# Feed-forward blocks of 512 tokens that run over the batch boundary, in a Fourier-mixing and ELU feed-forward kernel

## The chip, the core and the metric

The kernel runs on one core of a Trainium2 chip. A core has five engines that run beside each other: TensorE (PE, with its weight loads shown apart as PEld), VectorE (DVE), ScalarE (ACT), GpSimd (POOL) and SyncE (SP, which here only issues DMAs). Matrix products land in PSUM, from where DVE or ACT take them. The metric is the device time of one execution in microseconds.

## What is computed

The input is eight batches of 3,008 tokens with 256 features. Each batch goes through a Fourier transform along the tokens, a complex 256 x 256 product with bias, a soft threshold, and the inverse transform. The result, as 24,064 tokens in a row, goes through a feed-forward layer of 2,048 hidden features with an ELU.

```
X = rfft(x, axis=1)
Yr = Xr @ w_r - Xi @ w_i + b_r ;  Yi = Xr @ w_i + Xi @ w_r + b_i
Y* = sign(Y*) * max(|Y*| - 0.01, 0)
y = irfft(Yr + i Yi, n=3008, axis=1)
h = y.reshape(24064, 256) @ w_in
out = where(h > 0, h, exp(min(h, 0)) - 1) @ w_out
```

## The kernel before

**The transform** is done as matrix products, in units of work for one batch each:
- A (six units): first stage on the input tile `xt`; ACT copies the result out of PSUM, and after every second unit stores it to DRAM (`DA`).
- X (eight units): second stage, on `Z`, which SP loads from `DA`; ACT copies to `XT`.
- M (twelve units): the complex product; DVE adds the bias (L196), POOL does the soft threshold (L204, L205) into `Y`.
- B (six units): first stage of the inverse, from `Y`; ACT copies to `Bz` (L251), and after every second unit stores to DRAM (`DB`, L259).
- Y (eight units): last stage, from `Bs`, which SP loads from `DB` (`load_Bs`, L261, four loads, each for two Y units); ACT copies to `yT`, the transposed tokens of a batch, 752 tokens of one half of the features for each unit.

**The feed-forward** runs over blocks of up to 512 tokens, and for each block over eight pairs of 128 hidden features. One such pair is a *slot*, one turn of the loop at L826. A slot has a front, an ELU and a back:
- `front` (L675): four matmuls of `w_in_s` with 512 columns of `yT` into the PSUM tile `hps`; then ACT takes the exponential into `Et`. In a slot with an M unit ACT does two steps (L698, L699), in the others one (L701).
- `elu` and `finish_elu` (L706 to L727): DVE, with POOL in slots that hold no unit, clips `Et` and combines it with `hps` into `gT`. The combination is issued a slot later.
- `back` (L729): two slots after the front (LAG = 2), eight matmuls with 128 tokens of `gT` as the weights and `w_out_r` as the moving side, summed over the eight slots of a block in two PSUM tiles `ps_o`. After the eighth, ACT copies them to `osb` (L763, L767) and SP issues the output stores (L774). The next block uses the same two PSUM tiles.

A batch is cut into blocks by itself: 3,008 tokens are five blocks of 512 and one of 448, which are 48 slots (`PER`), 384 in all. In the block of 448 tokens the fronts have 448 columns and the eighth matmul of the back fills 64 rows of 128; all else is the same.

**The order of work** is written out by hand. While the feed-forward works on batch b, `plan(b)` (L783) lays one unit into a slot, ahead of the front: the rest of the Y units of batch b, then X, M and B of batch b+1, and A of batch b+2. The list `seq` starts at slot 0 (slot 1 for batch 0). With the two insertions, Y6 and Y7 stand at 20 and 24, M50 and M51 at 28 and 29, then A0, B4, A1, B5 and A2 to A5 at 30 to 37; A0 to A5 are dropped where there is no batch b+2. Y0 and Y1 of batch b+1 follow at slots 45 and 47 (`yn`). The `Bs` loads are issued in the slot of A2, the `Z` loads in that of A5, the input loads in slots 3, 8 and 13. All engines run their instructions in the order in which this loop issues them.

**PSUM**: two `hps` tiles (`psH`), one tile tagged `fps` (`psF`) that all units share, and the two `ps_o` tiles. In every third slot of a run of bare slots (slots without a unit) the front uses the `fps` tile as a third `hps`.

Of the kernel before, what the change touches and what calls it, by code (L numbers as in the profile page):

```python
# [9 lines left out]
AF = mybir.ActivationFunctionType  # L10
BF16 = mybir.dt.bfloat16
F32 = mybir.dt.float32
# [17 lines left out]
def kernel(  # L30
# [11 lines left out]
    nc = tc.nc  # L42
    P = nc.NUM_PARTITIONS

    B, S, D = x.shape
    assert D == 256 and S == N1 * N2
    DFF = moe_w_in.shape[1]
    E = moe_w_out.shape[1]
# [14 lines left out]
    w_in_s = constp.tile([P, 2, DFF], BF16, name="w_in_s")  # L63
# [24 lines left out]

    TB = 512
    NPAIR = NFT // 2  # L90
    NBLK = (S + TB - 1) // TB
    PER = NBLK * NPAIR
    LAG = 2
    n = B * PER
    WT = 2 * N1 * 8
# [10 lines left out]
    yT_of = {}  # L106
# [192 lines left out]
    with tc.tile_pool(name="stagep", bufs=1) as stagep:  # L299
# [12 lines left out]
        def mix(eng, a, sc, b, op0, op1, n=1):  # L312
            t = stagep.tile([P, n], F32, name=f"c{len(cols)}")
            cols.append(t)
            eng.scalar_tensor_tensor(t[:], a[:], sc, b[:], op0, op1)
            return t
# [73 lines left out]
        c1 = mix(dve, qcol, -2.0, pcol, ALU.mult, ALU.add)  # L390
        c0 = col(dve, c1, -1.0, ALU.mult, 1.0, ALU.add)
# [265 lines left out]
    for u in range(2):  # L657
# [9 lines left out]
    psO = ctx.enter_context(  # L667
        tc.tile_pool(name="psO", bufs=2, space=bass.MemoryType.PSUM, reuse_waits="tile")
    )
# [2 lines left out]
    g_of = {}  # L672
    po_of = {}

    def front(i, third, on_act):  # L675
        b, r = divmod(i, PER)
        blk, fp = divmod(r, NPAIR)
        bs = blk * TB
        nb = min(TB, S - bs)
        yT = yT_of[b]  # L680
        if third:
            hps = psF.tile([P, 2, TB], F32, name="hps", tag="fps")
        else:
            hps = psH.tile([P, 2, TB], F32, name="hps", tag="hps")
        for s in range(2):
            ft = 2 * fp + s
            for dt in range(2):
                nc.tensor.matmul(  # L688
                    hps[:, s, 0:nb], lhsT=w_in_s[:, dt, ft * P : ft * P + P],
                    rhs=yT[:, dt, bs : bs + nb], start=(dt == 0), stop=(dt == 1),  # L690
                )
        Et = late3.tile([P, 2, TB], F32, name="Et", tag="Et")
        E_ = Et[:, :, 0:nb]
        if i == n - 1:
            for s in range(2):
                nc.scalar.activation(E_[:, s], hps[:, s, 0:nb], AF.Exp)
        elif on_act:
            nc.scalar.activation(E_, hps[:, :, 0:nb], AF.Relu, scale=-1.0)  # L698
            nc.scalar.activation(E_, E_, AF.Exp, scale=-1.0)  # L699
        else:  # L700
            nc.scalar.activation(E_, hps[:, :, 0:nb], AF.Exp)  # L701
        return hps, Et, nb

    late_elu = []

    def finish_elu():  # L706
        for i, hps, Et, nb, whole in late_elu:
            E_, h_ = Et[:, :, 0:nb], hps[:, :, 0:nb]
            gT = late3.tile([P, 2, TB], F32R, name="gT", tag="gT")
            for s in range(2) if i == n - 1 else (slice(0, 2),):  # L710
                o, h, e = gT[:, s, 0:nb], h_[:, s], E_[:, s]
                if whole:
                    nc.vector.scalar_tensor_tensor(o, e, -1.0, h, ALU.add, ALU.max)  # L713
                else:
                    nc.vector.scalar_tensor_tensor(o, h, 0.0, e, ALU.max, ALU.add)  # L715
            g_of[i] = gT
        late_elu.clear()

    def elu(i, hps, Et, nb, on_pool, on_act):

        E_ = Et[:, :, 0:nb]
        if on_pool:
            for eng, s in ((nc.gpsimd, 1), (nc.vector, 0)):
                eng.tensor_scalar(E_[:, s], E_[:, s], 1.0, 0.0, ALU.min, ALU.max)  # L724
        elif not on_act:
            nc.vector.tensor_scalar(E_, E_, 1.0, -1.0, ALU.min, ALU.add)  # L726
        late_elu.append((i, hps, Et, nb, on_pool or on_act))  # L727

    def back(i):  # L729
        b, r = divmod(i, PER)  # L730
        blk, fp = divmod(r, NPAIR)
        bs = blk * TB
        nb = min(TB, S - bs)
        gT = g_of.pop(i)
        nsub = (nb + P - 1) // P
        if fp == 0:
            po_of[b, blk] = [
                psO.tile([P, 2, E], F32, name="ps_o", tag="outp") for _ in range((nsub + 1) // 2)
            ]
        po = po_of[b, blk]  # L740
        nq = (nsub + 1) // 2
        order = [(q, s) for q in range(nq) for s in range(2)]
        if i == n - 1:
            order = [(q, s) for s in range(2) for q in range(nq)]
        for q, s in order:
            ft = 2 * fp + s
            for i_ in range(2 * q, min(2 * q + 2, nsub)):
                t0, t1 = i_ * P, min(i_ * P + P, nb)
                nc.tensor.matmul(  # L749
                    po[q][0 : t1 - t0, i_ % 2, :], lhsT=gT[:, s, t0:t1],  # L750
                    rhs=w_out_r[:, ft, :], start=(ft == 0 and i_ % 2 == 0),
                    stop=(ft == NFT - 1), skip_group_check=True,
                )
        if fp < NPAIR - 1:
            return
        osb = late2.tile([P, 4, E], F32, name="osb", tag="osb")
        ov = out[b * S : b * S + S, :].rearrange("(r w j) e -> w r j e", w=4, j=8)
        last = i == n - 1
        for q in range(nq):
            k = min(2, nsub - 2 * q)  # L760
            copy = nc.vector.tensor_copy if last and q else nc.scalar.copy
            if nb >= (2 * q + k) * P:
                copy(osb[:, 2 * q : 2 * q + k, :], po[q][:, 0:k, :])  # L763
            else:
                for e in range(k):
                    rows = min(P, nb - (2 * q + e) * P)
                    copy(osb[0:rows, 2 * q + e, :], po[q][0:rows, e, :])  # L767
            for i_ in range(2 * q, 2 * q + k):
                t, end = bs + i_ * P, min(bs + i_ * P + P, bs + nb)
                while t < end:  # L770
                    w, r0 = t // WT, t % WT // 8
                    t1 = min(end, (w + 1) * WT)
                    p0, n8 = t - bs - i_ * P, (t1 - t) // 8
                    (nc.scalar if last and i_ % 2 == 0 else nc.sync).dma_start(  # L774
                        ov[w, r0 : r0 + n8], osb[p0 : p0 + 8 * n8, i_, :]
                    )
                    t = t1
        del po_of[b, blk]

    def put(kind, b, *a):  # L780
        return ({"A": unit_A, "X": unit_X, "M": unit_M, "B": unit_B, "Y": unit_Y}[kind], (b, *a))
# [1 line left out]
    def plan(b):  # L783

        f0 = [[] for _ in range(PER)]
        f1 = [[] for _ in range(PER)]
        n1, n2 = b + 1, b + 2
        mid = [("X", u) for u in range(8)] + [
# [4 lines left out]
        ]  # L793
        if n1 < B:
            lead, seq = int(b == 0), [("y", u) for u in range(2, 6)] + mid
            seq.insert(20, ("y", 6))
            seq.insert(24, ("y", 7))
            xs = (3, 8, 13)
            yn = (45, 47)
        else:  # L800
            lead, seq = 0, [("y", u) for u in range(2, 8)]
        for t, u in enumerate(seq, lead):
            if u[0] == "y":
                f0[t].append(put("Y", b, u[1]))
            elif u[0] == "A":
                if n2 < B:
                    f0[t].append(put("A", n2, u[1]))
            else:
                f0[t].append(put(u[0], n1, *u[1:]))
            if u == ("A", 2):  # L810
                f1[t] += [(load_Bs, (n1, w)) for w in range(4)]
            if u == ("A", 5) and n2 < B:
                f1[t] += [(load_Z, (n2, s0, s1)) for s0, s1 in ((0, 8), (8, NS))]
        if b == 0:
            f1[xs[0]].append((lambda: gate(Z_of[1][:, 16, 0:1]), ()))
        if n2 < B:
            for ci in range(3):
                f1[xs[ci]].append((load_x, (n2, ci)))
        if n1 < B:
            for u in range(2):  # L820
                f0[yn[u]].append(put("Y", n1, u))
        return f0, f1
# [3 lines left out]
    for i in range(n + LAG):  # L826
        if i < n:
            r = i % PER
            if r == 0:
# [7 lines left out]
            on_act = any(f is unit_M for f, a in f0[r])  # L837
            h = front(i, calm and bare % 3 == 2, on_act)
# [37 lines left out]
```

## Time and profile before

| | before |
|---|---|
| median of 3 runs | 941.27 us (941.2 to 941.69) |
| span of the profiled execution | 941.2 us |
| start of the slots, on PE | 59.5 us |
| slots | 384 |
| matmuls of the fronts (L688) | 1,536 |
| matmuls of the backs (L749) | 3,072 |
| HBM read and written | 55.31 MB, 49.81 MB |

The profile is of one execution. In its page and in the answers of the trace, a line such as `L749 PE MATMUL ps_o<-w_out_r,gT` names the line of the kernel, the engine, the operation, and what it writes and reads. "Busy" is the time in which an engine works on an instruction; matmuls overlap with each other, so a group's busy time is less than its count times the mean length of one, and the time from the start of one group to the start of the next tells better what it costs. In a timeline the columns are start and length in us, engine, line, operation, tiles, shapes and count, and in brackets the idle time of the engine ahead of it with what ended it.

### The profile page before, as it was taken

To read this page: it belongs to the slowest core of one execution; us is meant where nothing else is said; L and a number is where in the kernel's file an instruction comes from. 1 tells how busy PE (TensorE), PEld (TensorE's weight loads), DVE (VectorE), ACT (ScalarE), POOL (GpSimd) and SP (SyncE) were. 2 spreads that over 40 slices of the span, in tenths; PEclk is the share of its full clock that TensorE was granted. 3 is DMA by queue.
4 is the path that set the end of the run, shared out by engine and by line. 5 is a ranking of instruction groups with operands and counts; after the bars stand their busy time and mean duration, and the time that the engine had idled before them with its cause. 6 is when DMAs were issued, how large, how long until landed. Compare 5 with 4: busy or idle time off the path is not lost.

```text
span 941.2 us, 16753 instructions
## 1 busy us (share of the span) xinstructions
PE 914.0 (97%) x6583; PEld 644.5 (68%) x6583; DVE 735.0 (78%) x863; ACT 711.3 (76%) x818; POOL 265.6 (28%) x352
## 2 busy tenths in 40 slices
PE   8879999999999999999999999999999999999997
PEld 3447666776677666776667766777667766677775
DVE  7868677877788767886778866888678876788997
ACT  6657787787868788687787878778787878667664
POOL 6702430133310431205402143013331034221332
PEclk9999999999999999999999999999999999999999
DMA  8984217521283224722156021752128001321011
GB/s 261 362 235 142 85 46 216 163 68 46 90 224 109 68 64 122 213 92 88 49 170 206 27 90 45 208 170 68 45 82 232 23 23 55 106 65 42 23 46 43
DMA packets 90654, 106.20 MB, mean 113 GB/s; under 512 B 5264, under 2 KB 81296, under 8 KB 87216
## 3 DMA queue, kind: packets, MB, share of 16 engines
q1 hardware_dynamic: 43760, 57.16, 22.3%
q0 software_dynamic: 5968, 27.26, 8.9%
q10 hardware_dynamic: 40848, 20.71, 7.2%
q8 instruction: 51, 0.84, 0.4%
q14 instruction: 27, 0.22, 0.1%
HBM read 55.31 MB, written 49.81 MB: 112 GB/s over the span
## 4 chain that ended last, share of the span: by engine, by line
PE 49%; DVE 22%; ACT 17%; issue 5%; DMA 4%; ACTq 1%; DVEq 0%; POOL 0%; SPq 0%; POOLq 0%
PE hps L688 20%; PE ps_o L749 19%; DVE gT L713 10%; PE mps L189 5%; DVE gT L715 5%; ACT Et L701 5%; DVE Et L724 4%; ACT Et L698 3%; ACT osb L763 2%; ACT Bz L251 2%; DVE Et L726 2%; ACT A L126 2%; PE aps L143 2%; PE xps L174 2%; DVE yb L196 1%
## 5 line engine op out<-in xcount | busy, mean ns | idle before, releaser
L749 PE MATMUL ps_o<-w_out_r,gT 128*128 128x256 f32 (+1 forms) x3072 | 485.6, 301 | 1.3 <-DVE gT L713 0.5
L749 PEld LDWEIGHTS ps_o<-w_out_r,gT 128*128 128x128 f32 (+1 forms) x3072 | 405.9, 186 | 68.1 <-DVE gT L713 13.6
L688 PE MATMUL hps<-yT,w_in_s 128*128 128x512 bf16 (+1 forms) x1536 | 389.1, 375 | 8.8 <-DVE gT L715 5.0
L701 ACT ACTIVATE Et<-hps 128x1024 f32<-128x1024 f32 (+1 forms) x299 | 301.4, 1008 | 102.1 <-PE hps L688 81.1
L713 DVE SCALAR_TENSOR_TENSOR gT<-Et,hps 128x1024 fp32r<-128x1024 f32 (+2 forms) x187 | 220.0, 1177 | 62.3 <-ACT Et L699 44.7
L715 DVE SCALAR_TENSOR_TENSOR gT<-hps,Et 128x1024 fp32r<-128x1024 f32 (+1 forms) x198 | 240.2, 1213 | 17.6 <-DVE Et L726 0.9
L688 PEld LDWEIGHTS <-w_in_s 128*128 128x128 bf16 x1536 | 131.4, 98 | 146.8 <-issue 28.9
L726 DVE TENSOR_SCALAR Et<-Et 128x1024 f32<-128x1024 f32 (+1 forms) x198 | 136.0, 687 | 73.7 <-ACT Et L701 67.2
L204 POOL TENSOR_SCALAR clip<-yb 128x512 f32<-128x512 f32 x84 | 51.7, 616 | 339.2 <-DVE yb L196 277.9
L724 POOL TENSOR_SCALAR Et<-Et 128x512 f32<-128x512 f32 (+1 forms) x102 | 62.4, 612 | 280.6 <-ACT Et L701 279.4
L698 ACT ACTIVATE Et<-hps 128x1024 f32<-128x1024 f32 x84 | 86.5, 1029 | 67.5 <-PE hps L688 67.5
L205 POOL TENSOR_TENSOR Y<-yb,clip 128x512 bf16<-128x512 f32 x84 | 107.4, 1278 | 7.0
L196 DVE TENSOR_TENSOR yb<-mps,bias_bc 128x512 f32<-128x512 f32 x96 | 65.7, 688 | 34.3 <-PE mps L189 27.1
L699 ACT ACTIVATE Et<-Et 128x1024 f32<-128x1024 f32 x84 | 88.8, 1058 | 2.7
L126 ACT CAST XT<-xps 128x768 bf16<-128x768 f32 x61 | 49.1, 807 | 14.7 <-PE xps L174 14.7
L126 ACT CAST yT<-yps 128x752 bf16<-128x752 f32 x63 | 49.6, 788 | 13.2 <-PE yps L276 13.2
L189 PE MATMUL mps<-wcat_r,XT 128*128 128x512 bf16 x192 | 58.0, 384 | 0.6 <-ACT XT L126 0.6
L189 PE MATMUL mps<-wcat_s,XT 128*128 128x512 bf16 x192 | 57.1, 379 | 0.0
L724 DVE TENSOR_SCALAR Et<-Et 128x512 f32<-128x512 f32 (+1 forms) x102 | 56.1, 550 | 0.5 <-ACT Et L701 0.4
L126 ACT CAST A<-aps 128x1024 bf16<-128x1024 f32 x45 | 45.4, 1012 | 11.8 <-PE aps L143 11.6
L189 PEld LDWEIGHTS <-XT 128*128 128x128 bf16 x384 | 30.6, 98 | 29.5 <-ACT XT L126 0.9
L763 ACT COPY osb<-ps_o 128x512 f32<-128x512 f32 x88 | 47.2, 587 | 2.8 <-PE ps_o L749 2.8
(103 smaller groups left out, 400.5 us busy)
## 6 DMA issues: line engine op xcount, KB each, us to landing
xt<-in_x_dram POOLq DMA_DIRECT2D x21, 1024.0 KB, 5.4
out_dram<-osb SPq DMA_DIRECT2D x158, 128.0 KB
Bs<-DB SPq DMA_DIRECT2D x32, 384.0 KB
DB<-Bz ACTq DMA_DIRECT2D x21, 512.0 KB
DA<-A ACTq DMA_DIRECT2D x18, 512.0 KB
Z<-DA SPq DMA_DIRECT2D x7, 1152.0 KB
Z<-DA SPq DMA_DIRECT2D x11, 384.0 KB
xt<-in_x_dram POOLq DMA_DIRECT2D x6, 512.0 KB, 5.9
```

The lines of the kernel that those rows point to most:

```text
L126: nc.scalar.copy(dst, src)
L189: nc.tensor.matmul(ps, lhsT=XT[:, dt, c, o : o + P], rhs=wm[:, dt, :], start=(m == 0 and dt == 0), stop=(m == 1 and dt == 1),)
L205: nc.gpsimd.tensor_tensor(Y_of[b, q][:, i, :], yb[:], clip[:], ALU.subtract)
L688: nc.tensor.matmul(hps[:, s, 0:nb], lhsT=w_in_s[:, dt, ft * P : ft * P + P], rhs=yT[:, dt, bs : bs + nb], start=(dt == 0), stop=(dt == 1),)
L698: nc.scalar.activation(E_, hps[:, :, 0:nb], AF.Relu, scale=-1.0)
L699: nc.scalar.activation(E_, E_, AF.Exp, scale=-1.0)
L701: nc.scalar.activation(E_, hps[:, :, 0:nb], AF.Exp)
L713: nc.vector.scalar_tensor_tensor(o, e, -1.0, h, ALU.add, ALU.max)
L715: nc.vector.scalar_tensor_tensor(o, h, 0.0, e, ALU.max, ALU.add)
L724: eng.tensor_scalar(E_[:, s], E_[:, s], 1.0, 0.0, ALU.min, ALU.max)
L726: nc.vector.tensor_scalar(E_, E_, 1.0, -1.0, ALU.min, ALU.add)
L749: nc.tensor.matmul(po[q][0 : t1 - t0, i_ % 2, :], lhsT=gT[:, s, t0:t1], rhs=w_out_r[:, ft, :], start=(ft == 0 and i_ % 2 == 0), stop=(ft = ...
```

## The change

Blocks no longer end with a batch. The 24,064 tokens are cut into 47 blocks of 512, so there are 376 slots, and `PER`, the slots for each batch in the plan, is 47. A block that holds a batch boundary takes its front columns from two `yT` tiles: `pieces` cuts a stretch of tokens at the boundaries, and the front runs its matmuls for each piece, each with its own weight load, into the piece's columns of the same PSUM tile. There are seven such blocks; the pieces have 448 + 64, 384 + 128, 320 + 192, 256 + 256, 192 + 320, 128 + 384 and 64 + 448 tokens. The back always runs eight full matmuls. Output stores are cut at batch boundaries too.

In the plan, B4 and B5 move to slots 30 and 31, ahead of A0 to A5, which take 32 to 37; Y0 and Y1 of the next batch move to slots 38 and 39; the `Bs` loads move to the slot of A1 (33). Since 47 slots are not a multiple of 8, the ends of blocks fall on another slot of the plan in each batch.

```
-    NBLK = (S + TB - 1) // TB
-    PER = NBLK * NPAIR
+    assert S * NPAIR % TB == 0 and S % (P // 2) == 0
+    PER = S * NPAIR // TB
...
+    def pieces(t, k):
+
+        out_, c = [], 0
+        while c < k:
+            b, r = divmod(t + c, S)
+            e = min(k, c + S - r)
+            out_.append((b, r, c, e))
+            c = e
+        return out_
...
-        b, r = divmod(i, PER)
-        blk, fp = divmod(r, NPAIR)
-        bs = blk * TB
-        nb = min(TB, S - bs)
-        yT = yT_of[b]
+        blk, fp = divmod(i, NPAIR)
...
-            for dt in range(2):
-                nc.tensor.matmul(
-                    hps[:, s, 0:nb], lhsT=w_in_s[:, dt, ft * P : ft * P + P],
-                    rhs=yT[:, dt, bs : bs + nb], start=(dt == 0), stop=(dt == 1),
-                )
+            for b, t0, c0, c1 in pieces(blk * TB, TB):
+                for dt in range(2):
+                    nc.tensor.matmul(
+                        hps[:, s, c0:c1], lhsT=w_in_s[:, dt, ft * P : ft * P + P],
+                        rhs=yT_of[b][:, dt, t0 : t0 + c1 - c0],
+                        start=(dt == 0), stop=(dt == 1),
+                    )
...
-            for i_ in range(2 * q, min(2 * q + 2, nsub)):
-                t0, t1 = i_ * P, min(i_ * P + P, nb)
+            for i_ in range(2 * q, 2 * q + 2):
                 nc.tensor.matmul(
-                    po[q][0 : t1 - t0, i_ % 2, :], lhsT=gT[:, s, t0:t1],
+                    po[q][:, i_ % 2, :], lhsT=gT[:, s, i_ * P : i_ * P + P],
...
+            copy(osb[:, 2 * q : 2 * q + 2, :], po[q][:])
+            for i_ in range(2 * q, 2 * q + 2):
+                for b, t, c0, c1 in pieces(bs + i_ * P, P):
+                    ov = out[b * S : b * S + S, :].rearrange("(r w j) e -> w r j e", w=4, j=8)
+                    while c0 < c1:
+                        w, r0 = t // WT, t % WT // 8
+                        k = min(c1 - c0, (w + 1) * WT - t)
+                        (nc.scalar if last and i_ % 2 == 0 else nc.sync).dma_start(
+                            ov[w, r0 : r0 + k // 8], osb[c0 : c0 + k, i_, :]
+                        )
+                        t, c0 = t + k, c0 + k
...
-            ("M", 4, 1), ("B", 3), ("M", 5, 0), ("M", 5, 1), ("A", 0), ("B", 4), ("A", 1),
-            ("B", 5), ("A", 2), ("A", 3), ("A", 4), ("A", 5),
+            ("M", 4, 1), ("B", 3), ("M", 5, 0), ("M", 5, 1), ("B", 4),
+            ("B", 5), ("A", 0), ("A", 1), ("A", 2), ("A", 3), ("A", 4), ("A", 5),
...
-            yn = (45, 47)
+            yn = (38, 39)
...
-            if u == ("A", 2):
+            if u == ("A", 1):
                 f1[t] += [(load_Bs, (n1, w)) for w in range(4)]
```

More of the change, by code (lines that the diff above doesn't have):

```diff
@@ L686, in front @@
             ft = 2 * fp + s
-            for dt in range(2):
-                nc.tensor.matmul(
-                    hps[:, s, 0:nb], lhsT=w_in_s[:, dt, ft * P : ft * P + P],
-                    rhs=yT[:, dt, bs : bs + nb], start=(dt == 0), stop=(dt == 1),
-                )
+            for b, t0, c0, c1 in pieces(blk * TB, TB):
[5 more added lines that the diff above has]
+                    )
         Et = late3.tile([P, 2, TB], F32, name="Et", tag="Et")
-        E_ = Et[:, :, 0:nb]
+        E_ = Et[:]
         if i == n - 1:
             for s in range(2):
-                nc.scalar.activation(E_[:, s], hps[:, s, 0:nb], AF.Exp)
+                nc.scalar.activation(E_[:, s], hps[:, s], AF.Exp)
         elif on_act:
-            nc.scalar.activation(E_, hps[:, :, 0:nb], AF.Relu, scale=-1.0)
+            nc.scalar.activation(E_, hps[:], AF.Relu, scale=-1.0)
             nc.scalar.activation(E_, E_, AF.Exp, scale=-1.0)
         else:
-            nc.scalar.activation(E_, hps[:, :, 0:nb], AF.Exp)
-        return hps, Et, nb
+            nc.scalar.activation(E_, hps[:], AF.Exp)
+        return hps, Et
     late_elu = []
     def finish_elu():
-        for i, hps, Et, nb, whole in late_elu:
-            E_, h_ = Et[:, :, 0:nb], hps[:, :, 0:nb]
+        for i, hps, Et, whole in late_elu:
             gT = late3.tile([P, 2, TB], F32R, name="gT", tag="gT")
             for s in range(2) if i == n - 1 else (slice(0, 2),):
-                o, h, e = gT[:, s, 0:nb], h_[:, s], E_[:, s]
+                o, h, e = gT[:, s], hps[:, s], Et[:, s]
                 if whole:
@@ L717, in finish_elu, with elu @@
         late_elu.clear()
-    def elu(i, hps, Et, nb, on_pool, on_act):
-        E_ = Et[:, :, 0:nb]
+    def elu(i, hps, Et, on_pool, on_act):
+        E_ = Et[:]
         if on_pool:
@@ L726, in elu @@
             nc.vector.tensor_scalar(E_, E_, 1.0, -1.0, ALU.min, ALU.add)
-        late_elu.append((i, hps, Et, nb, on_pool or on_act))
+        late_elu.append((i, hps, Et, on_pool or on_act))
     def back(i):
-        b, r = divmod(i, PER)
-        blk, fp = divmod(r, NPAIR)
+        blk, fp = divmod(i, NPAIR)
         bs = blk * TB
-        nb = min(TB, S - bs)
         gT = g_of.pop(i)
-        nsub = (nb + P - 1) // P
+        nq = TB // P // 2
         if fp == 0:
-            po_of[b, blk] = [
-                psO.tile([P, 2, E], F32, name="ps_o", tag="outp") for _ in range((nsub + 1) // 2)
-            ]
-        po = po_of[b, blk]
-        nq = (nsub + 1) // 2
+            po_of[blk] = [
+                psO.tile([P, 2, E], F32, name="ps_o", tag="outp") for _ in range(nq)
+            ]
+        po = po_of[blk]
         order = [(q, s) for q in range(nq) for s in range(2)]
@@ L756, in back @@
         osb = late2.tile([P, 4, E], F32, name="osb", tag="osb")
-        ov = out[b * S : b * S + S, :].rearrange("(r w j) e -> w r j e", w=4, j=8)
         last = i == n - 1
         for q in range(nq):
-            k = min(2, nsub - 2 * q)
             copy = nc.vector.tensor_copy if last and q else nc.scalar.copy
[L762 to L778, printed above, removed]
+            copy(osb[:, 2 * q : 2 * q + 2, :], po[q][:])
[9 more added lines that the diff above has]
+                        t, c0 = t + k, c0 + k
+        del po_of[blk]
     def put(kind, b, *a):
```

## The prediction

> **What bounds the kernel now.** I read the busy shares first, then the windows of four stretches (each engine's busy time in them), then the timeline of PE, in which matmuls of one line that follow each other are merged: start, length, line, shape, count.
>
> ```profile
> PE 914.0 (97%) x6583; PEld 644.5 (68%) x6583; DVE 735.0 (78%) x863; ACT 711.3 (76%) x818; POOL 265.6 (28%) x352
> ```
>
> PE is busy for 97% of the span; no other engine is above 78%. A busy PE may still be waiting on its own pipeline, so the windows come next: batch 1's slots 0 to 37, its slots 38 to 47, then in the last batch the 34 slots of 512 tokens without a unit (slots 6 to 39), and six of its slots of 448 tokens (41 to 46). Columns: window, its length, busy us and count for each engine, granted PE clock, DMA.
>
> ```profile
> 172.80:266.36 93.56, 92.75 (x679) 65.66 (x677) 70.57 (x77) 76.61 (x88) 23.38 (x26) 1.00 0.33 98
> 266.36:284.94 18.58, 18.47 (x137) 14.04 (x136) 16.14 (x20) 12.27 (x15) 5.85 (x10) 1.00 0.68 185
> 856.36:919.51 63.15, 63.04 (x409) 45.00 (x408) 57.83 (x68) 38.50 (x43) 20.53 (x34) 1.00 0.13 34
> 921.20:931.54 10.34, 10.34 (x75) 7.83 (x73) 9.54 (x13) 6.41 (x9) 3.37 (x6) 1.00 0.19 51
> ```
>
> In each stretch PE is busy for 99 to 100% at full clock (1.00), with DVE second at 75 to 92%. So a slot costs what its matmuls cost, plus a stall here and there. The third and fourth rows give the price of a bare slot: 63.15/34 = 1.86 us at 512 tokens, 10.34/6 = 1.72 us at 448. (One odd slot at 917.32 takes 2.19; without it the full slot is 60.96/33 = 1.85, which I use.) The start times on PE split a slot into its parts:
>
> ```profile
> 858.15 1.04 PE L688 MATMUL hps<-yT,w_in_s 128*128 128x512 bf16 x4
> 858.84 1.27 PE L749 MATMUL ps_o<-w_out_r,gT 128*128 128x256 f32 x8
> 859.96 1.04 PE L688 MATMUL hps<-yT,w_in_s 128*128 128x512 bf16 x4
> ...
> 926.40 0.93 PE L688 MATMUL hps<-yT,w_in_s 128*128 128x448 bf16 x4
> 927.04 1.23 PE L749 MATMUL ps_o<-w_out_r,gT 128*128 128x256 f32 x8
> 928.11 0.93 PE L688 MATMUL hps<-yT,w_in_s 128*128 128x448 bf16 x4
> ```
>
> ```profile
> 186.04 0.52 PE L174 MATMUL xps<-M,Z 96*128 96x96 bf16 x8
> 186.40 1.03 PE L688 MATMUL hps<-yT,w_in_s 128*128 128x512 bf16 x4
> 187.07 1.27 PE L749 MATMUL ps_o<-w_out_r,gT 128*128 128x256 f32 x8
> 188.19 0.47 PE L174 MATMUL xps<-M,Z 96*128 96x96 bf16 x7
> ```
>
> ```profile
> 201.61 0.61 PE L189 MATMUL mps<-wcat_r,XT 128*128 128x512 bf16 x2
> ...
> 204.27 0.60 PE L189 MATMUL mps<-wcat_r,XT 128*128 128x512 bf16 x2
> ```
>
> An unstalled full slot takes 859.96 - 858.15 = 1.80 us. A slot with an X unit takes 188.19 - 186.04 = 2.15, so eight matmuls of 96 columns, each with its weight load, cost (2.15 - 1.80)/8 = 43 ns apiece. A slot with an M unit takes 2.66, so a matmul of 512 columns costs (2.66 - 1.80)/4 = 216 ns. From these two a matmul costs 3.5 ns + 0.415 ns a column. The front's four cost 0.86 us, which leaves 0.94 for the back's eight: 117 ns each. The 448-token slot still runs all eight (its last one fills 64 of 128 rows, at the same price) and takes 1.71.
>
> **The change, part by part.**
>
> *Eight slots fewer (376 for 384).* The front's columns are the same in all (24,064 tokens); what goes is the half-empty eighth matmul: 3,072 - 3,008 = 64 of them, 64 x 117 ns = 7.5 us of PE. I count it by stretches, so that stalls are in it.
> - Batches 1 to 5: slots 38 to 47 take 18.58 us in batch 1 and 18.54 to 18.57 in the others: seven bare slots short of stalls, one Y0 slot of 2.33 (278.83 to 281.17), one Y1 slot of 2.07. After: two full Y slots at 2.16 (284.94 to 287.10), seven bare full ones at 1.85, and 0.28 for the stall that Y0 meets on leaving the bare run (281.17 - 278.83 against 2.07), which the next batch's first Y now meets: 4.32 + 12.95 + 0.28 = 17.55. Gain 1.0 each, 5.0 in all.
> - Batch 0: slots 38 to 47 take 172.80 - 152.85 = 19.95. Here the list starts a slot late, so Y0 (slot 38) falls in the same slot as A5, and both use the one "fps" buffer. Y0 waits until ACT has copied A5 out: the copy ran from 153.50 to 154.51, while the PE would be free at 153.31: 1.2 us of wait and 0.35 of Y0, in a slot that already holds about 0.2 of stall: 3.85 for 2.45. After: 3.85 + 2.16 + 12.95 + 0.28 = 19.24. Gain 0.7.
> - Batch 6: 18.64 to 17.55, gain 1.1. Batch 7: from 856.36 to the end it takes 84.87 (34 full, 8 short slots and the output's tail). After: 40 x 1.85, and the last slot with its tail, which took 9.68 from 931.54 and grows by some 0.3 for 64 more tokens: 83.98. Gain 0.9.
> - Together 5.0 + 0.7 + 1.1 + 0.9 = 7.7. ACT's and DVE's shorter work (the third output copy of a 448-token block, L767, among it) lies beside PE.
>
> *Split fronts.* Seven blocks hold the end of one batch and the start of the next; each of their 56 slots runs 8 front matmuls for 4, 224 more: at 3.5 ns, 0.8 us. That is the lower end. In two of the blocks the piece has 64 columns (64 matmuls), below any row; if such a matmul costs no less than the 96-column one (43 ns instead of 30), 0.8 more. I take 1.2: the 96-column row is near, and shows the weight load hidden.
>
> The load of the weights is the dispute here: each of the 224 matmuls brings one, and its record lasts 98 ns. By the Trainium skill (TensorE: Matmul & The Clock Gate, LDWEIGHTS) a load takes its columns over 1.2 GHz, an estimate of 107 ns for 128 columns, which a short matmul couldn't cover; the same page (Weight-path perf modes) lets bf16 loads of 128 columns go about twice as fast. The X row's 43 ns for a load and its matmul sides with the second; by the first the short pieces (64, 128 and 192 columns, 64 matmuls each) would take 107 ns each and the sum would be 944, an estimate.
>
> *B4, B5 sooner; A0, A1 later; Y0, Y1 sooner.* The same units on the same engines, one a slot: nothing by themselves. What they wait for: B5 (slot 31) needs Y of M51 (slot 29). In the M slot that starts at 201.61 POOL ended its Y (L205) at 205.44, 3.8 us on; the two slots in between take 2.95 + 2.36 = 5.3. Y0 (slot 38) needs the first Bs load, which SP issues when B5's store has landed. Before, B5 ran at 253.83, ACT issued its store at 255.53, and SP issued the Bs loads at 260.22, behind four output stores (257.52): 6.4 us after B5. Give the first of four 384 KB loads 3 us (at the 200 KB a us that the queue moved there): 9.4 us. Now Y0 comes seven slots after B5, about 17 us, and 13 in batch 6, whose A slots are bare. Nothing waits, by 3.5 us at the least. The front that first needs Y0 and Y1 comes at slot 40 at the earliest; Y1's copy (0.79 us) ends inside slot 39.
>
> SP's queue: the four Bs loads move ahead of a block's output stores in some batches; those stores then leave some us later, but their tile has two buffers and is wanted again 8 slots (15 us or more) on. The two Z loads have 14 slots (27 us) until X0 where they had 15; their packets were through 6 us after the issue. ACT's queue: its DMA issues (0.37 us each) are as many. The number of output stores stays at 216.
>
> *Block ends move.* A block's two output copies (ACT, 0.59 us each) used to fall at slots 1, 9, 17, 25, 33, 41 of every batch. Blocks now drift by a slot each batch, so the copies meet other units. Before, in batch 1, they cost PE 0.33 us (slot 4), 0.0, 0.39 (slot 18), 0.39 (26), 0.40 (34) and 0.2 (40, 41): 0.29 on average. The wait can be read: the next block's first back needs them.
>
> ```profile
> PEld ps_o L749 <- ACT osb L763: 10.6, 25, 0.7
> ```
>
> After the change the ends lie over X, M, B, A, Y and bare slots much as before in number. I take no difference; the bounds are every end at 0.4 (47 x 0.4 - 48 x 0.29 = +4.9) and a third of the stall gone (-4.6).
>
> **Sum.** The profiled execution has a span of 941.2 us, as long as its median (941.27). 941.2 - 7.7 + 1.2 = 934.7 us.
>
> **Rivals.**
> - *Forecast*: PE gives back its 64 half-empty matmuls: 934.7, between 932 and 937. Chance 0.72.
> - *Copies in bad places*: every block end meets a unit that keeps ACT full (A, B or M: 2.0 to 2.1 us of ACT in a slot of 2.4 to 2.7): 934.7 + 4.9 = 939.6. For it: batches 1 to 6 each get a new place. Against: slots 18, 26 and 34 were already such places. Chance 0.13; the mirror of it (930) 0.05.
> - *Loads* (the slower side): the weight load of a short piece isn't hidden, and each short matmul takes what a back matmul with its load takes, 117 ns, in place of 30, 57 and 83 (64, 128 and 192 columns, 64 matmuls each): 64 x (87 + 60 + 34) = 11.6 us. 941.2 - 7.7 + 0.8 + 11.6 = 945.9. It decides the sign from 36 ns a short matmul on. Against it: the X row. At the 98 ns of the load's record it would be 942. Chance 0.06.
> - *Y0 waits for Bs*: seven batches at 1 us would give 941. It needs the way from B5 to Bs to take 18 us for the 9.4 read here. Chance 0.04.
>
> That the change fails to do what it says is out: the program after holds 3,008 back matmuls. From these: faster by over 0.2% (1.9 us, about what a measurement of this kernel can tell from no change) 0.86, within it 0.07, slower 0.07. The range 931 to 939.5 leaves out the slower cases and the ends of the copies' bounds.
>
> **What would show it.** In the profile after: slots of a split block at 1.80 to 1.90 us with x8 fronts (loads wrong if 2.1 or more where a piece is 64 wide); Y0 at slot 38 without an idle PE before it and no PE wait on the Bs DMA; in batch 0 about 1.2 us of idle PE between A5 and Y0; the wait of the back on the output copies near 10 us (copies wrong if 15); the last batch's bare slots at 1.85. I am wrong if bare full slots in the middle batches cost more than in the last one, or if stalls move by more than the 64 matmuls are worth.

## The result, and the profile after

The changed kernel takes 951.95 us (median of 5 runs) against 941.27: 1.0128 times as long, 95% interval 1.0107 to 1.015. The forecast was 934.7, faster. The profiled execution has a span of 949.9 us; its slots begin 1.9 us earlier in the record than before (57.6 us against 59.5), so the sum of the slots tells more than the span: 887.4 us after, 877.0 before, 10.5 more, close to the 10.7 between the medians.

On the page, PE is still the busiest engine, with 3.7 us less work than before (910.3 for 914.0) in a longer span:

```profile
PE 910.3 (96%) x6711; PEld 650.8 (69%) x6711; DVE 733.4 (77%) x846; ACT 710.2 (75%) x801; POOL 263.6 (28%) x345
```

The windows (length, then busy us and count of PE, PEld, DVE, ACT, POOL) are those of before: batch 1's slots 0 to 37, its slots from 38 on, and the last batch's bare slots 6 to 39.

```profile
170.04:266.44 96.40, 92.74 (x683) 65.94 (x681) 70.81 (x77) 76.63 (x87) 25.00 (x28) 1.00 0.34 105
266.44:284.43 17.99, 17.76 (x150) 14.48 (x149) 15.86 (x19) 12.27 (x14) 3.92 (x6) 1.00 0.55 147
865.68:928.84 63.16, 63.15 (x414) 45.24 (x414) 58.19 (x68) 38.41 (x43) 20.45 (x33) 1.00 0.13 34
```

The third row is what it was (63.15). The second fell from 18.58, though not to the 17.55 of the forecast. The first is where the time came from: 96.40 for 93.56, with the same 92.7 us of PE work, so PE now sits idle there. The waits of ACT name a line that the kernel before didn't have, and the waits of PE its consequence (waited for, total us, times, longest). The middle line, the back's wait on the output copies, stood at 10.6 before:

```profile
ACT A L126 <- DMA DA<-A: 11.1, 5, 3.0
PEld ps_o L752 <- ACT osb L763: 10.9, 22, 1.0
...
PEld aps L143 <- ACT A L126: 10.8, 5, 2.8
```

Batch 1 shows one of the five. First the timeline of ACT after, from A1's copy and store to A4's copy; then SP and PE in the same stretch; then ACT before.

```profile
253.33 1.01 ACT L126 CAST A<-aps 128x1024 bf16<-128x1024 f32 x1 [0.29 <-PE aps L143]
254.38 0.38 ACTq L156 DMA_DIRECT2D DA<-A  x1
...
260.13 1.02 ACT L709 ACTIVATE Et<-hps 128x1024 f32<-128x1024 f32 x1 [0.53 <-DVE gT L722]
263.00 1.01 ACT L126 CAST A<-aps 128x1024 bf16<-128x1024 f32 x1 [1.85 <-DMA DA<-A]
```

```profile
252.98 1.74 SPq L265 DMA_DIRECT2D Bs<-DB  x4
```

```profile
260.26 1.04 PE L695 MATMUL hps<-yT,w_in_s 128*128 128x512 bf16 x4
260.95 1.29 PE L752 MATMUL ps_o<-w_out_r,gT 128*128 128x256 f32 x8
264.07 0.73 PE L143 MATMUL aps<-xt,M 128*128 128x512 f32 x2 [1.83 <-ACT A L126]
```

```profile
253.08 0.37 ACTq L156 DMA_DIRECT2D DA<-A  x1
...
261.30 1.03 ACT L701 ACTIVATE Et<-hps 128x1024 f32<-128x1024 f32 x1 [0.56 <-ACT A L126]
262.21 1.01 ACT L126 CAST A<-aps 128x1024 bf16<-128x1024 f32 x1
```

A0 to A5 fill three tiles, and the tag "A" has two buffers: A4's copy writes into the buffer of A0 and A1, so it must wait until their store has landed. Before, the store left at 253.08, alone, the Bs loads were issued at 260.22, and A4's copy at 262.21 waited for nothing. After, SP issues the four Bs loads at 252.98, the store follows at 254.38, and A4's copy stands still until 263.00. PE waits behind it for the `fps` tile. The DMA view of the 4.6 us after the store's issue shows why the store is late (q1 is SP's queue, q10 ACT's: packets, MB, share of the 16 DMA engines):

```profile
q1 hardware_dynamic: 332, 1.18, 91.3%
q10 hardware_dynamic: 9, 0.00, 0.4%
```

The Bs loads take 91% of the time of the DMA engines, and the store gets 9 packets through; in the next 4 us it moves. The Trainium skill (DMA: Bandwidth & Descriptors, Issuing engines are not separate DMA queues) says that transfers issued by different engines run on the same 16 DMA engines and interleave. The first half agrees with the two shares; of interleaving, these 4.6 us show little.

Slot lengths, read from PE's start times and summed over all batches (us); the rows below the first give the difference to it, and the labels in brackets are the experiments that follow:

| kernel | slots 0-11 | 12-29 | 30-37 | from 38 | change of the sum |
|---|---|---|---|---|---|
| before | 207.6 | 365.6 | 151.4 | 152.3 | |
| after | +3.8 | +2.2 | +9.2 | -4.8 | +10.5 |
| old order (e3) | +3.6 | +1.6 | -1.0 | -5.6 | -1.3 |
| A4, A5 in Bz (e1b) | +3.8 | +2.2 | -2.1 | -5.3 | -1.5 |
| order only (e2) | -0.2 | +0.4 | +16.6 | +2.5 | +19.2 |
| Y0, Y1 sooner only (e9) | +0.5 | +0.1 | 0.0 | +3.5 | +4.2 |

Slots 36 and 37 of batches 1 to 5 alone went from 25.1 to 35.9 us.

### The profile page after: what moved, and what is told of

Its sections match the earlier page's. It is cut to its first block, busy times and chain, and to the rows that moved or that the text cites. A ratio compares the mean times of both kernels' runs of the same rounds, so it can differ in the third digit from the quotient of the medians.

```text
span 949.9 us, 16939 instructions
## 1 busy us (share of the span) xinstructions
PE 910.3 (96%) x6711; PEld 650.8 (69%) x6711; DVE 733.4 (77%) x846; ACT 710.2 (75%) x801; POOL 263.6 (28%) x345
## 4 chain that ended last, share of the span: by engine, by line
PE 46%; DVE 22%; ACT 13%; DMA 8%; issue 7%; POOL 2%; ACTq 1%; DVEq 0%; SPq 0%; POOLq 0%
PE hps L695 18%; PE ps_o L752 17%; DVE gT L720 11%; PE mps L189 6%; DMA DA<-A 6%; ACT Et L709 4%; DVE Et L731 4%; DVE gT L722 4%; ACT osb L763 2%; ACT Bz L251 2%; DVE Et L733 2%; ACT Et L706 2%; DMA Z<-DA 2%; ACT A L126 1%; PE xps L174 1%
## 5 line engine op out<-in xcount | busy, mean ns | idle before, releaser
L752 PE MATMUL ps_o<-w_out_r,gT 128*128 128x256 f32 x3008 | 472.5, 300 | 2.3 <-ACT osb L763 1.7
L752 PEld LDWEIGHTS ps_o<-w_out_r,gT 128*128 128x128 f32 x3008 | 398.6, 189 | 62.0 <-DVE gT L720 12.5
L695 PE MATMUL hps<-yT,w_in_s 128*128 128x512 bf16 (+7 forms) x1728 | 390.6, 354 | 11.8 <-DVE gT L722 6.7
L709 ACT ACTIVATE Et<-hps 128x1024 f32<-128x1024 f32 x291 | 300.1, 1031 | 105.4 <-PE hps L695 84.3
L720 DVE SCALAR_TENSOR_TENSOR gT<-Et,hps 128x1024 fp32r<-128x1024 f32 x180 | 218.1, 1212 | 58.1 <-ACT Et L707 41.7
L722 DVE SCALAR_TENSOR_TENSOR gT<-hps,Et 128x1024 fp32r<-128x1024 f32 x197 | 240.8, 1222 | 17.2 <-PE hps L695 0.5
L695 PEld LDWEIGHTS <-w_in_s 128*128 128x128 bf16 x1728 | 145.2, 98 | 147.2 <-issue 34.5
L733 DVE TENSOR_SCALAR Et<-Et 128x1024 f32<-128x1024 f32 x197 | 136.3, 692 | 90.2 <-ACT Et L709 84.2
L731 POOL TENSOR_SCALAR Et<-Et 128x512 f32<-128x512 f32 x95 | 60.4, 636 | 299.6 <-ACT Et L709 298.4
L706 ACT ACTIVATE Et<-hps 128x1024 f32<-128x1024 f32 x84 | 86.4, 1028 | 66.4 <-PE hps L695 66.4
L731 DVE TENSOR_SCALAR Et<-Et 128x512 f32<-128x512 f32 x95 | 54.2, 571 | 0.4 <-ACT Et L709 0.2
```

The costliest lines, as they stand in the source:

```text
L695: nc.tensor.matmul(hps[:, s, c0:c1], lhsT=w_in_s[:, dt, ft * P : ft * P + P], rhs=yT_of[b][:, dt, t0 : t0 + c1 - c0], start=(dt == 0), sto ...
L706: nc.scalar.activation(E_, hps[:], AF.Relu, scale=-1.0)
L709: nc.scalar.activation(E_, hps[:], AF.Exp)
L752: nc.tensor.matmul(po[q][:, i_ % 2, :], lhsT=gT[:, s, i_ * P : i_ * P + P], rhs=w_out_r[:, ft, :], start=(ft == 0 and i_ % 2 == 0), stop=( ...
```

## Experiments

**Store theory**: the new order of units puts the Bs loads ahead of A1's store, and A4 waits for that store. **Blocks theory**: the split fronts and the drifting block ends cost the time. I first undid or did one part at a time. The kernel before was run again beside each experiment, and each ratio is against those runs (medians 941.88 us for e2 and e3, 942.25 for e1b, e5 and e7, 942.38 for e8 and e9).

**The order alone** (e2): the kernel before with

```
-("A", 0), ("B", 4), ("A", 1), ("B", 5), ("A", 2), ...
+("B", 4), ("B", 5), ("A", 0), ("A", 1), ("A", 2), ...
...
-            if u == ("A", 2):
+            if u == ("A", 1):
                 f1[t] += [(load_Bs, (n1, w)) for w in range(4)]
```

> The kernel before (48 blocks, cut at the batch) with only the new order of units: B4 and B5 ahead of A0 to A5, the Bs loads in the slot of A1; Y0 and Y1 stay at 45 and 47. Store theory: slots 36 and 37 grow here too, by about 2 us in each of batches 1 to 5, and the time is 949 to 953. Blocks theory: 940 to 943, since no block is split or moved.

Measured: 960.15 us, 1.0186 times before (1.0169 to 1.0203). The order alone does it, and costs more than in the changed kernel and more than the 949 to 953 expected: slots 36 and 37 take 7.9 to 9.6 us in each of batches 1 to 5 (43.1 us in all). Why the wait is longer here stays open. The wait of ACT:

```profile
ACT A L126 <- DMA DA<-A: 15.2, 5, 3.6
```

**The old order in the changed kernel** (e3): the reverse of that diff; blocks and Y0, Y1 as changed.

> The changed kernel with the old order of A and B units (A0, B4, A1, B5, A2 to A5) and the Bs loads back in the slot of A2; blocks over the boundary and Y0, Y1 at 38 and 39 stay. Store theory: the store of A1 is issued before the Bs loads again, A4 doesn't wait, 938 to 943, unless Y0 now waits for Bs (some 9 us after B5, which stands 5 slots ahead, 12 us: no wait, or 1 us in batch 6). Blocks theory: 950 to 953.

Measured: 940.91 us, 0.9992 times before (0.9982 to 1.0003), with no wait of ACT for that store. Slots 36 and 37 are back at 24.4 us in all. The blocks theory falls as the cause of the loss. But the blocks' gain is mostly missing too, which the later experiments take up.

**The wait alone** (e1b): the changed kernel in its new order, with the third A tile elsewhere. SBUF had no room for a third A buffer of its own (e1_three_a, which gave no time: the pool of `Et` and `gT` needs 24 KB a partition, and 19.8 were left), so the third tile takes one of the two `Bz` buffers.

```
-                A_of[b, ci] = wk2.tile([P, 8, D], BF16, name="A", tag="A")
+                t = "Bz" if ci == 2 else "A"
+                A_of[b, ci] = wk2.tile([P, 8, D], BF16, name=t, tag=t)
```

> The changed kernel with A4 and A5 in a tile of the Bz pair in place of the A pair, whose store left several slots earlier; nothing else is changed. Store theory: the copy of A4 no longer waits for the store of A0 and A1, slots 36 and 37 of batches 1 to 5 return to about 5.0 us, and the time is 938 to 942. Rival (the wait only shows a delay of PE that would appear elsewhere, since A units in a row keep ACT full): 947 or more.

Measured: 941.21 us, 0.9986 (0.9976 to 0.9996), slots 36 and 37 at 24.6 us. The order of the units, the Bs loads and the late store are all still there; only the copy no longer needs that store. So the loss is this one wait.

**The loads later** (e5): the changed kernel, with

```
-    def load_Bs(b, w):
+    def load_Bs(b, w, eng=None):
...
-        nc.sync.dma_start(Bs[:], dv[:, 8 * w : 8 * w + 8, :])
+        (eng or nc.sync).dma_start(Bs[:], dv[:, 8 * w : 8 * w + 8, :])
...
-            if u == ("A", 1):
-                f1[t] += [(load_Bs, (n1, w)) for w in range(4)]
+            if u == ("A", 3):
+                if n2 < B:
+                    f1[t].append((lambda: gate(A_of[n2, 1][:, 7, 0:1]), ()))
+                f1[t] += [(load_Bs, (n1, w, nc.gpsimd)) for w in range(4)]
```

> The changed kernel with its order of units and its two A tiles, but the Bs loads are issued by POOL's queue behind a small copy that reads A3's result, so about two slots after A1's store was issued in place of just ahead of it. If the store is late because the Bs loads are ahead of it in the DMA engines: the store lands within some 4 us, A4 doesn't wait, 938 to 944 (up to 2 us in batch 6 or elsewhere if Y0 now waits for Bs). If the one slot less between A1 and A4 is what makes the wait: 948 or more, with A4's wait as before.

Measured: 950.55 us, 1.0086 (1.0065 to 1.0106). The time fits the second case of the expectation and the profile the first. ACT has no wait for the store any more, though A4 still comes only three slots behind A1: so the Bs loads ahead of the store made it late, and not the lost slot. The time came back in another place, which the waits of PE tell:

```profile
PEld L276 <- DMA Bs<-DB: 10.9, 7, 3.3
...
PE yps L276 <- DMA Bs<-DB: 9.1, 6, 2.9
```

Y0 at slot 38 now waits for Bs (in batch 1 the first load was issued at 264.88, 5.9 us after A1's store, and landed at 272.35). In the new order, with two A tiles and Y0 at slot 38, each of the two places tried for the loads made something late, the store or the loads themselves; in the old order (e3) neither is late.

**The price of a split front** (e4, e6): the kernel before, with the fronts of the last batch's second to fourth block split at 64, 128 and 256 columns; in e4 the first columns run first, in e6 last. The edit of e4 (e6 takes the two pieces in the other order):

```
-            for dt in range(2):
+            cut = (64, 128, 256)[blk - 1] if b == B - 1 and blk in (1, 2, 3) else nb
+            for c0, c1 in ((0, cut), (cut, nb))[: 1 + (cut < nb)]:
+                for dt in range(2):
...
```

> The kernel before, with the fronts of three full blocks of the last batch (bare slots) split at column 64, 128 and 256: the price of a split front by itself. By the 96-column row 16 to 66 ns a slot at 64 and 16 ns at 128 and 256; by the trace after (1.87 to 1.88 for 1.80) 75 ns in all three, 1.8 us in 24 slots; with weight loads unhidden at 98 ns 0.3 us a slot at 64 and 0.2 at 128.

> The kernel before with the fronts of three full blocks of the last batch split as in e4, but with the piece of 64, 128 and 256 columns last in place of first. If the split costs more where the last piece is short (the first weight load of the back, 188 ns, has only that piece to hide under): slots without another stall at about 1.88 us at 64 and 1.87 at 128, against 1.83 with the short piece first, and 1.83 at 256. If the order makes no difference: 1.83 in all.

Measured in one execution each, as the mean slot of each block (64, 128, 256): whole 1.853, 1.847, 1.854 us; short piece first 1.859, 1.852, 1.854; short piece last 1.910, 1.887, 1.851. So a split costs 6 ns a slot or less with the short piece first, and 58 and 39 ns with it last. In e4 the slots without a stall rose from 1.80 to about 1.83 us, but the stalls of their neighbours shrank, so the mean hardly moved. In e6 single slots read 1.88 to 1.92 at 64 and 1.89 at 128. The weight loads of the back (start, length) say what differs. First PEld in the kernel with the short piece last, then in a slot of the kernel before:

```profile
864.69 0.93 PEld L690 LDWEIGHTS <-w_in_s 128*128 128x128 bf16 x8
865.55 1.01 PEld L751 LDWEIGHTS ps_o<-w_out_r,gT 128*128 128x128 f32 x8
```

```profile
858.15 0.55 PEld L688 LDWEIGHTS <-w_in_s 128*128 128x128 bf16 x4
...
858.82 1.10 PEld L749 LDWEIGHTS ps_o<-w_out_r,gT 128*128 128x128 f32 x8
```

The front's stream takes 0.86 us. In this whole front, in a slot without a stall, the back's first load starts 0.67 us in, under the last matmul; with 64 columns last it starts at 0.86, when the stream is over. That fits a load that has only a short matmul to hide under; it isn't tested by itself.

**Y0 and Y1 sooner, alone** (e9): the kernel before with `yn = (38, 39)`.

> The kernel before (48 blocks, cut at the batch, old order of A and B units) with Y0 and Y1 of the next batch moved from slots 45 and 47 to 38 and 39: the move alone. If the part of the gain that e3 lacks went into the two Y units right behind the A units, and into the first Y after a longer bare run: slots 38 and 39 take 4.5 to 5.5 us together where two Y slots of 2.16 were reckoned, and the time is 943 to 946. If the move is free: 940 to 941.5, and the gain went into the split fronts and the block ends alone.

Measured: 945.73 us, 1.0036 (1.0023 to 1.005). The move costs 4.2 us in the profile's slots by itself. Eight bare slots now stand in a row, and the plan gives them no third `hps` at the end, since it keeps `fps` free two slots ahead of the next Y. PE of batch 1, at the end of the run:

```profile
280.44 0.93 PE L688 MATMUL hps<-yT,w_in_s 128*128 128x448 bf16 x4
281.09 1.20 PE L749 MATMUL ps_o<-w_out_r,gT 128*128 128x256 f32 x8
282.80 0.92 PE L688 MATMUL hps<-yT,w_in_s 128*128 128x448 bf16 x4 [0.50 <-DVE gT L713]
```

That slot takes 282.80 - 280.44 = 2.36 us where a bare one takes 1.71: its successor's front waits for DVE to free one of two `hps` tiles. No run gives that slot a third tile. And Y1's slot takes 2.57 us in this batch, where 2.16 was reckoned for a Y slot.

**Y0 and Y1 spread out** (e7): e3 with the short piece first and

```
-            yn = (38, 39)
+            yn = (38, 39) if b == 0 else (39, 40) if b == 1 else (39, 41)
```

> The changed kernel with the old order of A and B units and the Bs loads in A2's slot (as in e3), the short piece of a split front first, and Y0 and Y1 moved from slots 38 and 39 to 39 and 40 in batch 1 and to 39 and 41 in batches 2 to 6, so that a bare slot follows A5 and another stands between the two. If what e3 lost against the sum of the prediction sits in those two Y slots (2.4 to 3.3 us for 2.16) and in short last pieces: 936 to 938. If it sits in the block ends that meet other units: 940.

Measured: 946.02 us, 1.0035 (1.0025 to 1.0045): neither case of the expectation, and slower than both. Its profile shows a granted clock of 0.85, where no other here has less than 0.98, so its slot lengths can't be set beside the others. Why it is slower stays open, and with it where the rest of e3's missing gain sits.

**A faster version** (e8): e3 with the short piece of a split front first.

```
-            for b, t0, c0, c1 in pieces(blk * TB, TB):
+            for b, t0, c0, c1 in sorted(pieces(blk * TB, TB), key=lambda p: p[3] - p[2]):
```

> The changed kernel with the old order of A and B units and the Bs loads in A2's slot (as in e3), and the short piece of a split front first. If a short last piece costs 50 to 80 ns a slot because the first weight load of the back can't hide under it: the bare split slots of batches 0 to 2 fall from 1.87-1.88 us to 1.83, some 1.0 to 1.5 us in all, and the time lies at 939 to 940, below the kernel before. If the piece's place doesn't matter here: 941, as e3.

Measured: 940.81 us, 0.9983 (0.9973 to 0.9993): 0.2% faster than the kernel before, and 0.1 us from e3's median, so just outside the 939 to 940 expected. The bare split slots of batches 0 and 1 fell from 1.88 and 1.87 us to 1.84 and 1.86 on average, about half of what was expected.

## Why the prediction was wrong

**The step that failed** is the one headed "B4, B5 sooner; A0, A1 later; Y0, Y1 sooner", which put these moves at "nothing by themselves". It listed who waits for B5, Y0, Z and the output stores, and not who waits for A's own stores. SP's queue was weighed for what the Bs loads delay on SP; what they delay in the DMA engines, the store that ACT issues 1.4 us later, was left out, and with it the buffer that A4 needs. Sized at 0, the wait of A4's copy costs 10.8 us (slots 36 and 37 of batches 1 to 5), as e2, e3 and e1b show from three sides. No rival had it, but the last sign of being wrong came true: stalls that moved by more than the 64 matmuls are worth (7.5 us). The reading of the windows shares in it: "DVE second" holds in three of the four, but in batch 1's slots 0 to 37, where the loss arose, ACT is second (76.61 of 93.56 us, 82%; DVE has 75%). (The count of seven bare slots in 38 to 47 should be eight; the sum doesn't use it.)

**Without that wait** the rest of the change gives -1.3 to -1.5 us in slots (e3, e1b) where the sum had -6.5. By its terms:
- *Eight slots fewer.* Right in kind. From the move of Y0 and Y1 alone (e9, +4.2) to that move with the blocks (e3, -1.3) is 5.5 us, near the 6.5 of the forecast with its split fronts; that is a difference of two kernels, not a run by itself. Bare full slots cost 1.86 in the last batch, as before, and 1.83 to 1.86 on average in slots 40 to 46 of batches 1 to 6, where 1.85 was reckoned, and batch 0's slot of A5 and Y0 took 3.86 for 3.85.
- *Y0 and Y1 sooner.* Reckoned as 4.32 us for the two slots; in batches 1 to 6 they take 4.5 to 5.5 (e3), and the first Y of the next batch stalls by 0.44 (2.60 for 2.16) where 0.28 was put. These two, 3.8 + 1.1 us, are as much as nearly all of the missing gain. e9, without any change of blocks, loses 3.5 us in its slots from 38; but its two Y slots take 4.7 to 4.8 us together in batches 3 and 4, where e3's take 5.4 to 5.5, so a part of the 3.8 comes only with the moved blocks, and how isn't shown.
- *Block ends.* Taken as no difference; slots 12 to 29 grew by 1.6 (e3) to 2.2 us, inside the bounds. The end now meets an M slot with a B slot behind it in some batches: in batch 1 slots 19 and 27 take 3.22 us for 2.37, and slots 18 and 26 ahead of them 2.75 for 3.05 (e3). The rival "copies" is out by the sign set for it: the back's wait on the output copies is 10.9 us, where 15 would have spoken for it.
- *Split fronts.* 1.2 us for 56 slots is 21 ns a slot; the measured 0 to 58 ns (e4, e6) depends on which piece runs last. The rival "loads" (0.2 us or more a slot) is out; its milder form, a load without cover, shows in the back.
- *Y0's wait for Bs* didn't occur in the changed kernel, as reckoned (PE's one wait on Bs, 1.1 us, comes at 55.7 us, ahead of the slots). It does in e5.

## What to carry to other kernels

When a step is moved, list for each of its DMAs not only who waits for it, but which transfers it now runs ahead of, and whose buffers those hold: a store is a wait for the next writer of its tile. A bound from PE's work holds only as long as the other engines' buffers keep their distance; a saved 117 ns matmul is worth nothing where a copy waits 2 us for a store. Where loads would go ahead of a store, look whose tile that store frees: here another buffer for the next writer (e1b) and the old order (e3) each took the wait away.

## What the runs showed that I had not expected

- A 512 KB store with packets of 512 bytes moved 9 packets in 4.6 us while 1.5 MB of loads with packets of 4 KB ran in the other queue; the copy that waited for it went on 8.6 us after its issue.
- The place of the short piece: 64 columns last cost 58 ns a slot, first 6 ns.
- At the end of a run of bare slots, where only two `hps` tiles are in use, a slot took 2.36 us for 1.71, with PE idle for 0.50 us until DVE freed a tile.
